# Attention's value products of two heads side by side in TensorE's columns, softmax sums as products of their own

## The chip, the cores and the metric

The kernel runs on one core of a Trainium2 chip. The metric is the device time of one execution in microseconds (us), as the median of several runs. Engines are named as in the profile: PE is TensorE (matmuls; PEld are its weight loads), DVE is VectorE, ACT is ScalarE, POOL is GpSimd, SP is SyncE, which here issues nearly all transfers (DMAs).

## The reference

Three layers follow each other. Inputs: 4 batches, 8 heads, 576 positions, 64 values a head; 32 heads in all.

```python
def _attn_ref(q, k, v, f):
    scores = scale * np.matmul(q, k.transpose(0, 1, 3, 2))
    cum = np.cumsum(np.log(np.clip(f, 0.0001, 1.0)), axis=-1)
    decay = cum[:, :, :, None] - cum[:, :, None, :]
    scores = np.where(causal, -1000000000.0, scores + decay)
    scores = scores - np.max(scores, axis=-1, keepdims=True)
    attn = np.exp(scores)
    attn = attn / (np.sum(attn, axis=-1, keepdims=True) + 1e-09)
    return np.matmul(attn, v)

def _moe_ref(x, w_in, w_spatial, b_spatial, w_out):       # x: heads side by side, 512 columns
    h = np.maximum(x @ w_in, 0.0)
    u, v = h[..., :512], h[..., 512:]
    v_n = (v - mean(v)) / np.sqrt(var(v) + 1e-06)
    v_s = np.einsum('ts,bsd->btd', w_spatial, v_n) + b_spatial[None, :, None]
    return (u * v_s) @ w_out

def _moe2_ref(x, mu_k, mu_r, w_k, w_v, w_r):
    xk, xr = mixes of x and x shifted by one position
    k = np.maximum(xk @ w_k, 0.0)
    return 1.0 / (1.0 + np.exp(-(xr @ w_r))) * (k * k @ w_v)
```

## The kernel before

Heads are worked in pairs: pair p holds heads 2p and 2p+1 (`g` is a head's number, 0 to 31). For each pair q and k are loaded, split into half-precision parts and transposed by DMA. For each head `score` and `rowmax` find the row maxima, and `scoreT` (L328) computes the scores once more, transposed, with keys on the partitions; ACT's exponential writes them to the tile `e`, 128 x 1600 f32. It holds, one behind the other, the five blocks of 128 keys (the last has 64), each with the queries that may see it: 576, 448, 320, 192 and 64 columns, starting at `EO`. `causal` (L341) clears on POOL what lies above the diagonal.

`pv` (L346) multiplies with the values, in f32. For each block c of keys, the stationary operand is 128 columns of the tile `v`, in which 64 columns of ones stand between the values of an even and of an odd head. So one product gives on 64 partitions of `o` the 64 outputs of the head, and on the other 64 its softmax sums. It is done in two halves of the queries, 0 to 255 (two products, of 256 and 128 columns) and 256 to 575 (five, of 320, 320, 320, 192 and 64). `o` is one PSUM tile of two banks, with one buffer, and serves one head.

`head` (L359) copies `o` to `xo` with ACT and sends the row of sums to the DRAM tile `rd`. Once a pair, `recip` (L370) brings the sums of both heads back with 9 to a partition, takes reciprocals on DVE, sends them to DRAM and spreads them over the partitions (`sr`). `norm` (L383) multiplies on POOL, one instruction a head; `xhi` and `xlo` split the result into two half-precision parts `xt`, on which the next layer's products work (m1v L504, m1u L558, m2 L575). These are done for batch b while the attention of batch b+1 runs; what is left of attention and of this layer runs out after 390 us, and from 445 us the last layers' products fill PE (L715).

Order: `plan_attention` (L611) gives each step a due time from the table `P` (L31), in units of a head, and a priority; the steps are written down in the order of these times, and a scheduler then settles the order of the instructions on each engine, while it keeps tiles and buffers free of conflicts. What it settles is fixed in the program. Due times of a head g are `pv` g+1.0 and g+1.3, `head` g+1.35; of a pair, counted from its odd head, `recip` 1.4, `norm` 1.9, `xhi` 2.2, `xlo` 2.4.

Of the kernel before, what the change touches and what calls it, by code (L numbers as in the profile page):

```python
# [29 lines left out]

P = dict(load=-8.0, sq=-5.6, ss=-5.2, sc=-5.0, hik=-4.6, lok=-4.25, hiq=-4.2, loq=-3.95, aux=-3.6,  # L31
         s=-2.4, m=-0.65, t=0.0, pv=1.0, out=1.35, rc=1.4, nr=1.9, xs=2.2, xl=2.4, mlp=2.7, mlplen=7.0, vload=-5.0, vsq=-3.0,
# [7 lines left out]
class K:  # L40
# [68 lines left out]
    def setup(self):  # L109
# [35 lines left out]
        self.v = [at.tile([128, 5, 4, 192], F32, name=f"v{i}") for i in range(2)]  # L145
# [19 lines left out]
    def init(self, i):  # L165

        g = self.nc.gpsimd
        if i < 3:
            for nm in ("kT", "kA"):
                g.memset(self.T[nm, i][:, 10], 0.0)  # L170
            t = self.T["kA", i].rearrange("p c t -> p (c t)")
            g.memset(t[64:69, 0:1280], MS)
            for h in range(2):
                g.memset(t[64:69, 640 * h:640 * h + 64], 0.0)
        elif i < 5:

            t = self.v[i - 3]
            x = g.memset(t[:, :, :, 64:128], 1.0)
            if i == 4:
                self.pin(x)  # L180
            g.memset(t[64:128, 4], 0.0)
        elif i == 5:
            for nm in "kq":
                g.memset(self.nat[nm, 2][0:64, :, 0, :], 0.0)
        else:
            self.pin(g.memset(self.xt[i - 6][:, :, 576:640], 0.0))
# [31 lines left out]
    def vload(self, b, c):  # L218
        t, src = self.v[b % 2], self.a["v"][b]
        t0, tn = KB[c]  # L220
        for e in range(2):
            self.nc.sync.dma_start(t[:tn, c, :, 128 * e:128 * e + 64], src[e::2, t0:t0 + tn].rearrange("h p d -> p h d"))

    def vsq(self, b, c):
        if c == 0:
            self.va = self.at.tile([128, 16], F32, tag="va", bufs=2, name="va")
        t = self.v[b % 2][:, c].rearrange("p a (x d) -> p a x d", d=64)[:, :, 0:3:2]
        self.sumsq(self.va[:, c:c + 1], t, self.junka[:, 0:512].rearrange("p (a x d) -> p a x d", a=4, x=2))
# [99 lines left out]
    def scoreT(self, g, u):  # L328
# [8 lines left out]
        if u == 0:  # L337
            self.e[g] = self.at.tile([128, 1600], F32, tag="e", bufs=2, name="e")
# [7 lines left out]
    def pv(self, g, hf):  # L346

        b, h = divmod(g, 8)
        if hf == 0:
            self.o[g] = self.pso.tile([128, 1024], F32, tag="o", name="o")  # L350
        o, e, v = self.o[g], self.e[g], self.v[b % 2]
        q0, q1 = ((0, 256), (256, 576))[hf]
        cs = [c for c in range(5) if KB[c][0] < q1]
        for c in cs:
            f = max(q0, KB[c][0])
            off = EO[c] + f - KB[c][0]
            self.nc.tensor.matmul(o[:, 256 + f:256 + q1], v[:, c, h // 2, 64 * (h % 2):64 * (h % 2) + 128], e[:, off:off + q1 - f], start=(c == 0), stop=(c == cs[-1]))  # L357

    def head(self, g):  # L359

        nc = self.nc
        o = self.o.pop(g)
        h = g % 2
        t = self.xo[h] = self.at.tile([128, 576], F32, tag="xo", bufs=3, name="xo")
        nc.scalar.copy(t, o[:, 256:832])
        if h == 0:
            self.rd = [self.hl.tile([2, 576], F32, tag=f"rd{i}", bufs=2, name=f"rd{i}") for i in range(2)]
        nc.sync.dma_start(self.rd[0][h:h + 1], t[64 - 64 * h:65 - 64 * h])
# [14 lines left out]
    def norm(self, p):  # L383

        self.xp = self.at.tile([128, 576], F32, tag="x", bufs=2, name="x")
        for h in range(2):
            r = slice(64 * h, 64 * h + 64)
            self.nc.gpsimd.tensor_tensor(self.xp[r], self.xo[h][r], self.sr[r], ALU.mult)  # L388
# [222 lines left out]
    def plan_attention(self):  # L611
# [21 lines left out]
        for g in range(G):  # L633
# [4 lines left out]
            for hf in range(2):  # L638
                add(g + P["pv"] + 0.3 * hf, 5, self.pv, g, hf)
            add(g + P["out"], 1, self.head, g)  # L640
            if g % 2:
                add(g + P["rc"], 1, self.recip, g // 2)
# [230 lines left out]
```

## Time and profile before

| | us |
|---|---|
| median of 3 runs | 752.72 (752.52 to 752.82) |
| profiled execution, first to last instruction | 750.9 |
| PE busy | 674.9 (90%) |
| DVE busy | 426.8 (57%) |
| ACT busy | 372.2 (50%) |
| POOL busy | 184.5 (25%) |
| L357, the value products on PE: 448 matmuls | 114.0 |
| L388, the norm's products on POOL: 32 | 47.0 |

The busy time of PE counts each matmul from its start to the end of its way through the array, so that the times of matmuls close behind each other overlap; what a matmul costs its successor is read from the distance of their starts. An f32 product is carried out as two matmuls (passes), each with its own weight load, so the 224 products of `pv` stand in the profile as 448.

### The profile page before, as it was taken

Reading aid. Unit: us, or ns where it says so; the run is one execution under the profiler, and the core shown is the slowest. Engines: PE = TensorE matmul, PEld = TensorE weight load, DVE = VectorE, ACT = ScalarE, POOL = GpSimd, SP = SyncE. Lnnn points to the kernel's source line nnn. Section 1 sums busy time; section 2 is a strip of 40 time slices with the busy share of each in tenths; the row PEclk is TensorE's granted clock in tenths of the full one; section 3 lists DMA queues with packets and bytes.
Section 4 is the critical chain, followed back from the end, with each engine's and each line's share of the span. In section 5 each row is a group of like instructions: output and inputs, shape, how many; then the busy total and the mean of one; then the engine's idle time right before and its main releaser. Section 6 shows DMA issues by size and latency. Waiting matters only on the chain.

```text
span 750.9 us, 11016 instructions
## 1 busy us (share of the span) xinstructions
PE 674.9 (90%) x3718; PEld 499.5 (67%) x3718; DVE 426.8 (57%) x1147; ACT 372.2 (50%) x740; POOL 184.5 (25%) x385
## 2 busy tenths in 40 slices
PE   0377878989998999999997679999999999999997
PEld 0245545647775677666774458788888888888886
DVE  5987786666655656646026879988225512632342
ACT  4626786666426854355505539747225412622431
POOL 7122645555324544445321201000000000000000
PEclk9998968999999999999999899999999999999999
DMA  9997666765655234410025453450100100010010
GB/s 228 203 204 158 168 138 131 147 137 107 126 133 122 56 71 99 97 27 18 18 64 184 146 192 124 140 164 15 42 27 16 57 0 15 1 56 1 1 57 28
DMA packets 130681, 69.78 MB, mean 93 GB/s; under 512 B 114704, under 2 KB 115312, under 8 KB 130624
## 3 DMA queue, kind: packets, MB, share of 16 engines
q1 hardware_dynamic: 128032, 67.89, 37.1%
q10 hardware_dynamic: 2592, 1.19, 0.7%
q8 instruction: 29, 0.48, 0.3%
q14 instruction: 28, 0.23, 0.1%
HBM read 42.06 MB, written 9.79 MB: 69 GB/s over the span
## 4 chain that ended last, share of the span: by engine, by line
PE 60%; DMA 16%; DVE 10%; POOL 5%; issue 3%; ACT 3%; SPq 1%; DVEq 0%; ACTq 0%; POOLq 0%
PE m L715 40%; PE o L357 7%; DMA sr<-rd 3%; POOL x L388 3%; PE m L575 3%; PE m1v L504 3%; PE s L302 3%; PE t L335 2%; PE m1u L558 2%; DMA rd<-r 2%; DVE junk L311 2%; DMA r<-rd 2%; DMA wst<-in_moe_w_k_dram 1%; DMA rd<-xo 1%; DMA wst<-in_moe_w_in_dram 1%
## 5 line engine op out<-in xcount | busy, mean ns | idle before, releaser
L357 PE MATMUL o<-e,v 128*128 128x320 f32 (+4 forms) x448 | 114.0, 384 | 5.5 <-POOL e L344 3.7
L715 PE MATMUL m<-xx,moe_w_k 128*128 128x512 f32 (+1 forms) x480 | 107.5, 373 | 0.4 <-ACT x L710 0.4
L715 PE MATMUL m<-moe_w_v,k 128*128 128x512 f32 x432 | 104.8, 391 | 0.0
L339 ACT ACTIVATE e<-t,qa 128x512 f32<-128x512 f32 (+1 forms) x128 | 72.6, 590 | 50.4 <-PE t L335 50.1
L311 DVE CUSTOM_DVE_ANT_0 junk<-s,mask 128x512 bf16<-128x512 f32 (+4 forms) x160 | 75.9, 474 | 37.8 <-PE s L302 32.2
L715 PEld LDWEIGHTS m<-xx,moe_w_k 128*128 128x128 f32 x480 | 84.0, 188 | 18.1 <-ACT x L710 0.9
L357 PEld LDWEIGHTS o<-e,v 128*128 128x128 f32 x448 | 78.5, 199 | 23.7 <-POOL e L344 6.1
L715 PEld LDWEIGHTS m<-moe_w_v,k 128*128 128x128 f32 x432 | 80.7, 188 | 17.7
L344 POOL TENSOR_SCALAR_AFFINE_SELECT e<-e 128x128 f32<-128x128 f32 (+1 forms) x160 | 52.2, 342 | 125.5 <-ACT e L339 123.0
L751 DVE TENSOR_TENSOR tmp<-tmp 128x512 f32<-128x512 f32 (+1 forms) x40 | 25.5, 638 | 88.1 <-ACT tmp L750 87.9
L302 PE MATMUL s<-kT,qT 128*128 128x512 f16 (+2 forms) x192 | 55.8, 299 | 21.6 <-DVE nm L311 13.7
L504 PE MATMUL m1v<-win,xt 128*128 128x512 f16 x240 | 61.5, 397 | 0.0
L388 POOL TENSOR_TENSOR x<-xo,sr 64x576 f32<-64x576 f32 x32 | 47.0, 1469 | 47.6 <-DMA sr<-rd 46.4
L715 PE MATMUL m<-gh,moe_w_out 128*128 128x512 f32 (+1 forms) x240 | 55.1, 380 | 3.5 <-DVE u L578 3.5
L335 PE MATMUL t<-qA,kA 69*128 69x512 f16 (+2 forms) x192 | 51.6, 294 | 7.3 <-DMA qA<-md 6.7
L558 PE MATMUL m1u<-xt,win 128*128 128x288 f16 x384 | 53.6, 286 | 4.5 <-ACT u L560 4.5
L750 ACT ACTIVATE tmp<-m 128x512 f32<-128x512 f32 (+1 forms) x40 | 22.1, 556 | 71.6 <-PE m L715 71.4
L575 PE MATMUL m<-wspT,vn 128*128 128x288 f16 x384 | 54.4, 290 | 3.0 <-DVE u L578 2.3
L302 PE MATMUL s<-kA,qA 67*128 67x512 f16 (+2 forms) x192 | 50.6, 300 | 4.0 <-DMA kA<-kT 3.7
L701 POOL COPY x<-x 128x4 f32<-128x4 f32 x4 | 3.5, 884 | 198.1 <-ACT x L710 198.1
L715 PEld LDWEIGHTS m<-gh,moe_w_out 128*128 128x128 f32 x240 | 43.3, 193 | 13.0 <-DVE u L578 3.8
L335 PE MATMUL t<-qT,kT 128*128 128x512 f16 (+2 forms) x192 | 51.4, 293 | 0.0
(159 smaller groups left out, 1083.8 us busy)
## 6 DMA issues: line engine op xcount, KB each, us to landing
sr<-rd SPq DMA_DIRECT2D x32, 144.0 KB
gd<-u SPq DMA_DIRECT2D x16, 288.0 KB
out_dram<-o SPq DMA_DIRECT2D x18, 256.0 KB
knat<-in_k_dram SPq DMA_DIRECT2D x32, 128.0 KB
v<-in_v_dram SPq DMA_DIRECT2D x32, 128.0 KB
g<-gd SPq DMA_DIRECT2D x16, 256.0 KB
wst<-in_moe_w_k_dram SPq DMA_DIRECT2D x8, 512.0 KB
wst<-in_moe_w_v_dram SPq DMA_DIRECT2D x8, 512.0 KB
```

The source lines that it names most:

```text
L302: self.nc.tensor.matmul(s[:, o:o + n], self.tok(qn, p, h, 128 * ib - 64, 128)[0:r], self.tok(kn, p, h, k0, n)[0:r], start=(j == 0), stop=( ...
L311: self.nc.vector.tensor_tensor_reduce(out=self.junk[r0:, 0:n], in0=self.s[u % 2][r0:, o:o + n], in1=self.mask[r0:, m0:m0 + n], op0=ALU.add ...
L335: self.nc.tensor.matmul(t[:, o:o + n], self.tok(kn, p, h, 128 * c, 128)[0:r], self.tok(qn, p, h, q0, n)[0:r], start=(j == 0), stop=(j == 1))
L339: self.nc.scalar.activation(self.e[g][:, 512 * u:512 * u + n], t[:, 0:n], AF.Exp, scale=self.qa[p][:, 5:6])
L344: self.nc.gpsimd.affine_select(out=e, in_=e, pattern=[[1, n]], compare_op=ALU.is_ge, fill=0.0, base=0, channel_multiplier=-1)
L357: self.nc.tensor.matmul(o[:, 256 + f:256 + q1], v[:, c, h // 2, 64 * (h % 2):64 * (h % 2) + 128], e[:, off:off + q1 - f], start=(c == 0), ...
L388: self.nc.gpsimd.tensor_tensor(self.xp[r], self.xo[h][r], self.sr[r], ALU.mult)
L504: nc.tensor.matmul(self.m1p, xt[:, xs, 128 * j:128 * j + 128], self.win[:, ws, kc, 512:1024], start=(kc == 0 and n == 0), stop=(kc == 3 an ...
L558: self.nc.tensor.matmul(o, self.win[:, ws, kc, fs], self.xt[(4 * b + kc) % 8][:, xs, ts_], start=(kc == 0 and n == 0), stop=(kc == 3 and n ...
L575: nc.tensor.matmul(o, pairs[n][0], pairs[n][1], start=(n == 0), stop=(n == 13))
L715: self.nc.tensor.matmul(out, l, r, start=(first and j == 0), stop=(last and j == len(pairs) - 1))
L751: nc.vector.tensor_tensor(tmp[:, 0:n], tmp[:, 0:n], tmp[:, 0:n], ALU.mult)
```

## The change

The two heads of a pair are now multiplied together, after the second one's exponentials. The values of a head are 64 stationary columns; head 2p is placed in the left half of the array's columns and writes partitions 0 to 63 of `o`, head 2p+1 in the right half and writes partitions 64 to 127. `o` holds a pair now. The softmax sums are products of their own: the stationary operand is 32 columns of ones, in one of four strips of 32 columns, two for each head. Which block, which queries and which place in `o` a strip works on stands in the table `SUMS`: each row is (block, first query, end, column of `o`), for strip j = 0 or 1 of a head. They use the columns of the two PSUM banks that the values leave free.

`e` has three buffers instead of two. `head` copies 864 columns once a pair, and four transfers bring the sums to `rd`. `norm` is one instruction on 128 partitions. `v` has no ones, and one transfer loads a block instead of two. The due times of `head`, `recip`, `norm`, `xhi` and `xlo` move back.

```diff
+SUMS = ((((0, 288, 480, 832),), ((1, 288, 480, 832),), ((2, 288, 480, 832),), ((3, 384, 480, 928),), ((0, 0, 96, 160),)),
+        (((0, 96, 288, 832),), ((1, 128, 288, 864),), ((0, 480, 576, 160), (1, 480, 576, 160)), ((2, 480, 576, 160),), ((3, 480, 576, 160),), ((4, 512, 576, 192),), ((2, 256, 288, 992),)))
...
-         s=-2.4, m=-0.65, t=0.0, pv=1.0, out=1.35, rc=1.4, nr=1.9, xs=2.2, xl=2.4, mlp=2.7, mlplen=7.0, vload=-5.0, vsq=-3.0,
+         s=-2.4, m=-0.65, t=0.0, pv=1.0, out=1.65, rc=1.7, nr=2.15, xs=2.35, xl=2.42, mlp=2.7, mlplen=7.0, vload=-5.0, vsq=-3.0,
...
-        self.v = [at.tile([128, 5, 4, 192], F32, name=f"v{i}") for i in range(2)]
+        self.v = [at.tile([128, 5, 8, 64], F32, name=f"v{i}") for i in range(2)]
...
-        for e in range(2):
-            self.nc.sync.dma_start(t[:tn, c, :, 128 * e:128 * e + 64], src[e::2, t0:t0 + tn].rearrange("h p d -> p h d"))
+        self.nc.sync.dma_start(t[:tn, c], src[:, t0:t0 + tn].rearrange("h p d -> p h d"))
...
-            self.e[g] = self.at.tile([128, 1600], F32, tag="e", bufs=2, name="e")
+            self.e[g] = self.at.tile([128, 1600], F32, tag="e", bufs=3, name="e")
...
-    def pv(self, g, hf):
-
-        b, h = divmod(g, 8)
-        if hf == 0:
-            self.o[g] = self.pso.tile([128, 1024], F32, tag="o", name="o")
-        o, e, v = self.o[g], self.e[g], self.v[b % 2]
-        q0, q1 = ((0, 256), (256, 576))[hf]
-        cs = [c for c in range(5) if KB[c][0] < q1]
-        for c in cs:
-            f = max(q0, KB[c][0])
-            off = EO[c] + f - KB[c][0]
-            self.nc.tensor.matmul(o[:, 256 + f:256 + q1], v[:, c, h // 2, 64 * (h % 2):64 * (h % 2) + 128], e[:, off:off + q1 - f], start=(c == 0), stop=(c == cs[-1]))
-
-    def head(self, g):
-
-        nc = self.nc
-        o = self.o.pop(g)
-        h = g % 2
-        t = self.xo[h] = self.at.tile([128, 576], F32, tag="xo", bufs=3, name="xo")
-        nc.scalar.copy(t, o[:, 256:832])
-        if h == 0:
-            self.rd = [self.hl.tile([2, 576], F32, tag=f"rd{i}", bufs=2, name=f"rd{i}") for i in range(2)]
-        nc.sync.dma_start(self.rd[0][h:h + 1], t[64 - 64 * h:65 - 64 * h])
+    def pv(self, p, part):
...
+        b = p // 4
+        mm = self.nc.tensor.matmul
+        if part == 0:
+            self.o[p] = self.pso.tile([128, 1024], F32, tag="o", name="o")
+        o, v = self.o[p], self.v[b % 2]
+
+        def probs(h, c, q0, q1):
+            off = EO[c] + q0 - KB[c][0]
+            return self.e[2 * p + h][:, off:off + q1 - q0]
+
+        if part < 2:
+            q0, q1 = ((0, 256), (256, 576))[part]
+            cs = [c for c in range(5) if KB[c][0] < q1]
+            for c in cs:
+                f = max(q0, KB[c][0])
+                for h in range(2):
+                    mm(o[64 * h:64 * h + 64, 256 + f:256 + q1], v[:, c, 2 * (p % 4) + h], probs(h, c, f, q1), start=(c == 0), stop=(c == cs[-1]))
+            return
+        ones = self.ones[:, 0:32]
+        for i in range(7):
+            for h in range(2):
+                for j in range(2):
+                    if j == 0 and i > 4:
+                        continue
+                    for c, q0, q1, at in SUMS[j][i]:
+                        r = 64 * h + 32 * j
+                        mm(o[r:r + 32, at:at + q1 - q0], ones, probs(h, c, q0, q1), start=(c == 0), stop=(q1 - 1) // 128 == c, tile_position=(0, r))
+
+    def head(self, p):
+
+        nc = self.nc
+        t = self.xo[p] = self.at.tile([128, 864], F32, tag="xo", bufs=2, name="xo")
+        nc.scalar.copy(t, self.o.pop(p)[:, 160:1024])
+        self.rd = [self.hl.tile([2, 576], F32, tag=f"rd{i}", bufs=2, name=f"rd{i}") for i in range(2)]
+        for r, q, n, at in ((0, 0, 96, 0), (32, 480, 96, 0), (0, 288, 192, 672), (32, 96, 192, 672)):
+            nc.sync.dma_start(self.rd[0][:, q:q + n], t[r:128:64, at:at + n])
...
-        for h in range(2):
-            r = slice(64 * h, 64 * h + 64)
-            self.nc.gpsimd.tensor_tensor(self.xp[r], self.xo[h][r], self.sr[r], ALU.mult)
+        self.nc.gpsimd.tensor_tensor(self.xp, self.xo.pop(p)[:, 96:672], self.sr, ALU.mult)
...
-            for hf in range(2):
-                add(g + P["pv"] + 0.3 * hf, 5, self.pv, g, hf)
-            add(g + P["out"], 1, self.head, g)
             if g % 2:
+                for part in range(3):
+                    add(g + P["pv"] + 0.2 * part, 5, self.pv, g // 2, part)
+                add(g + P["out"], 1, self.head, g // 2)
```

What this moves on PE, in the second batch's part of the program (pair 9, heads 18 and 19). Before, the end of head 19's products; `e_2595` is its tile of exponentials, `o_2767` its output, and a row with "x2" stands for two products:

```order
L302 LDWEIGHTS qA2_138
L302 MATMUL s_2818<-kA2_136,qA2_138 128x64
L357 MATMUL o_2767<-e_2595,v0_139 128x320 x2
L357 MATMUL o_2767<-e_2595,v0_139 128x192
L357 MATMUL o_2767<-e_2595,v0_139 128x64
L558 LDWEIGHTS win_103
```

After, at the same place of the program, the values of both heads; `e_2649` belongs to head 18, `e_2792` to head 19, and `o_2948` is the pair's output:

```order
L366 MATMUL o_2948<-e_2649,v0_139 64x320
L366 MATMUL o_2948<-e_2792,v0_139 64x320
L366 MATMUL o_2948<-e_2649,v0_139 64x320
L366 MATMUL o_2948<-e_2792,v0_139 64x320
L366 MATMUL o_2948<-e_2649,v0_139 64x192
L366 MATMUL o_2948<-e_2792,v0_139 64x192
L366 MATMUL o_2948<-e_2649,v0_139 64x64
L519 LDWEIGHTS xt6_147
```

And, some twenty matmuls of the next layer later, the beginning of the pair's sums:

```order
L376 MATMUL o_2948<-e_2649,ones_121 32x192 x2
L376 MATMUL o_2948<-e_2792,ones_121 32x192 x2
L376 MATMUL o_2948<-e_2649,ones_121 32x192
L376 MATMUL o_2948<-e_2649,ones_121 32x160
L376 MATMUL o_2948<-e_2792,ones_121 32x192
L376 MATMUL o_2948<-e_2792,ones_121 32x160
```

The products of the two heads now alternate, and the sums follow as a run of narrow products. Earlier in the same pair the first product, of 256 columns of head 18, stands alone between full-width matmuls of L335.

On SP's queue, before, the end of the same pair: two transfers of L368, of 576 sums each, with transposes and copies of other pairs between them, then the way through DRAM.

```order
L368 DMA rd_2669<-xo 1x576
L325 DMA md<-mr 20x128
L326 DMA qA_134<-md 2x1280
L272 DMA_TRANSPOSE kT_127<-nk 128x10x128
L272 DMA_TRANSPOSE qT_129<-nq 128x10x128
L278 DMA kA_128<-kT_127 64x1280
L279 DMA kA_128<-cumd 3x1280
L284 DMA qA_130<-qT_129 64x1280
L368 DMA rd_2669<-xo 1x576
L375 DMA r_2846<-rd_2669 128x9
L378 DMA rd_2670<-r_2846 128x9
L381 DMA sr<-rd_2670 64x576 x2
```

After, the same pair's sums:

```order
L385 DMA rd_3095<-xo 2x96 x2
L385 DMA rd_3095<-xo 2x192 x2
L392 DMA r_3106<-rd_3095 128x9
L395 DMA rd_3096<-r_3106 128x9
L398 DMA sr<-rd_3096 64x576 x2
```

All four transfers of a pair's sums now stand directly ahead of the one that waits for them.

## Rows read from the trace of the kernel before

**Rows 1.** The page's busy times, shares of the span and instructions of each engine.
```profile
PE 674.9 (90%) x3718; PEld 499.5 (67%) x3718; DVE 426.8 (57%) x1147; ACT 372.2 (50%) x740; POOL 184.5 (25%) x385
```
**Rows 2.** Three stretches: length, busy us and instructions by engine, granted clock, DMA.
```profile
core 0: us, PE busy (x) PEld busy (x) DVE busy (x) ACT busy (x) POOL busy (x), PEclk, DMA share, GB/s
0.00:125.00 125.00, 78.55 (x398) 49.84 (x399) 97.92 (x336) 76.89 (x167) 54.67 (x118) 0.90 0.82 177
125.00:400.00 275.00, 265.66 (x1750) 181.38 (x1749) 141.66 (x470) 136.40 (x279) 118.44 (x239) 0.98 0.42 92
400.00:751.00 351.00, 330.70 (x1573) 268.27 (x1571) 187.25 (x341) 158.90 (x294) 11.43 (x29) 0.99 0.19 64
```
**Rows 3.** Waits, 125 to 400 us: who for whom, total us, times, longest.
```profile
ACT e L339 <- PE t L335: 33.0, 29, 4.5
...
PE s L302 <- DVE nm L311: 3.5, 5, 2.3
...
PE o L357 <- POOL e L344: 2.4, 1, 2.4
...
PE t L335 <- ACT e L339: 0.2, 1, 0.2
```
**Rows 4.** The stretches again, line 357 alone: PE and PEld busy.
```profile
0.00:125.00 125.00, 32.29 (x112) 21.32 (x112) 0.90 0.82 177
125.00:400.00 275.00, 81.75 (x336) 57.15 (x336) 0.98 0.42 92
```
**Rows 5.** Timeline of PE from 347.2 us: start, us, line, operation, count.
```profile
347.30 0.19 PE L302 MATMUL s<-kT,qT 128*128 128x64 f16 x1
347.33 0.19 PE L302 MATMUL s<-kA,qA 67*128 67x64 f16 x1
347.36 2.35 PE L357 MATMUL o<-e,v 128*128 128x320 f32 x10
349.55 0.41 PE L558 MATMUL m1u<-xt,win 128*128 128x288 f16 x2
```
**Rows 6.** Timeline of PE from 261.9 us.
```profile
262.25 0.28 PE L71 MATMUL tot<-qa,ones 128*128 128x2 f32 x2
262.39 0.30 PE L302 MATMUL s<-kT,qT 128*128 128x320 f16 x1
```
**Rows 7.** Chain that ended last, from 378 us: start, us, what; the last pair.
```profile
384.94 2.87 DMA sr<-rd
387.82 0.07 issue
387.89 1.41 POOL x L388
389.30 0.07 issue
389.36 1.41 POOL x L388
390.77 0.02 issue
390.79 0.68 ACT xt L391
391.47 0.07 issue
391.54 1.29 POOL xt L395
```
**Rows 8.** ACT's group of the head's copy; SP's issue of the last sums.
```profile
L365 ACT COPY xo<-o 128x576 f32<-128x576 f32 x32 | 20.2, 633 | 26.0 <-PE o L357 22.3 <-POOL x L388 3.4
...
379.90 0.24 SPq L368 DMA_DIRECT2D rd<-xo  x1
```
**Rows 9.** Narrowest form of line 357: busy us, mean ns.
```profile
L357 PE MATMUL o<-e,v 128*128 128x64 f32 x64 | 11.0, 254 | 0.0
```

More of the change, by code (lines that the diff above doesn't have):

```diff
@@ L175, in init @@
         elif i < 5:
-            t = self.v[i - 3]
-            x = g.memset(t[:, :, :, 64:128], 1.0)
+            x = g.memset(self.v[i - 3][64:128, 4], 0.0)
             if i == 4:
                 self.pin(x)
-            g.memset(t[64:128, 4], 0.0)
         elif i == 5:
@@ L226, in vsq @@
             self.va = self.at.tile([128, 16], F32, tag="va", bufs=2, name="va")
-        t = self.v[b % 2][:, c].rearrange("p a (x d) -> p a x d", d=64)[:, :, 0:3:2]
-        self.sumsq(self.va[:, c:c + 1], t, self.junka[:, 0:512].rearrange("p (a x d) -> p a x d", a=4, x=2))
+        self.sumsq(self.va[:, c:c + 1], self.v[b % 2][:, c].rearrange("p h d -> p (h d)"), self.junka[:, 0:512])
     def vscale(self, b):
```

## The prediction

> **What bounds the kernel now.** I read the page's busy times first: TensorE (PE) is busy 90% of the span, the next engine 57% [rows 1]. A share over the whole span hides the stages, so the second view is the busy time of three stretches [rows 2]. Up to 125 us PE works 78.55 of 125 us and waits for loads and scaling. From 125 to 400 us it works 265.66 of 275 us at a granted clock of 0.98, and what it does wait for there is a handful of short waits, the longest group 3.5 us [rows 3]. After 400 us nothing of attention runs. So between 125 and 400 us attention is bounded by the columns that PE streams, and a microsecond added to PE or taken from it there moves the end of attention by about as much. The third view says how much of the changed line lies there: 336 of its 448 matmuls, 112 lie earlier [rows 4].
>
> What one of these matmuls costs must not be taken from its mean duration, since matmuls overlap in the pipeline. It is taken from starts. Every f32 product stands in the trace as two passes, each with its own weight load (448 for 224 products). Ten passes of one head (six of 320 columns, two of 192, two of 64: 2432 columns) start at 347.36 and the next line's matmul starts at 349.55 [rows 5]: 2.19 us, 0.90 ns a column. The full-width weight loads hide behind these streams. Starts are one behind the other in the order of the program, also where the second pass of a product follows its first.
>
> **Value products, L357.** Before, a head streams 1600 columns (256, 128, three of 320, 192, 64) twice: 3200, and 102,400 for 32 heads, times 0.90 ns = 92.2 us of PE. After, the same 102,400 columns are streamed, each into half of the array's columns. One at a time they cost 92.2 us again; two abreast 46.1 us.
>
> **Sums.** They came for nothing with the value products, as the 64 columns of ones beside v. Now they are 26 products a pair, 416 in all, 832 passes; the table's pieces add up to 768 + 832 = 1600 columns a head, so another 102,400 columns: 92.2 us one at a time, 46.1 us two abreast, 23.0 us four abreast.
>
> **How many abreast?** No row of before shows a matmul that leaves part of the array's columns free, so this is bounded from both sides: one at a time 184.4 us against 92.2 (+92.2), four abreast for the sums and two for the values 69.1 us (-23.1). I take two abreast for both. The reason is the order in which passes start: the second pass of a product goes into the same strip as its first, so it waits until that has streamed, and the product for the next strip stands behind it in the queue. What then runs together is the second pass of one product and the first of the next, two and never four. Net: 46.1 + 46.1 - 92.2 = 0.
>
> **Stretches.** Abreast needs a neighbour. The order of the changed kernel breaks its narrow products into 97 stretches with full-width matmuls between them, 21 of them of a single product; the first product of a stretch has 206 columns on average, and its first pass has nobody beside it: 97 x 206 x 0.90 ns = 18.0 us. In the pair shown, the values of 320 columns alternate well, while its first product of 256 stands alone.
>
> **Weight loads.** Passes narrower in columns but as many, and 832 more, bring 1280 loads for 448. Two passes of 2 columns, which hide no load, took 0.14 us from start to start of the next line [rows 6]; a pass of 64 columns behind another takes 0.03 us [rows 5], so a bare load of 128 columns is about 0.11 us. By columns (an estimate) 0.055 us for 64 and 0.028 us for 32. If the first load of each product waits for the pass before it to start, 224 x 0.055 + 416 x 0.028 = 24 us are added; if it is made early, nothing, as now behind the streams. I take the middle, 12 us.
> The Trainium skill (TensorE: Matmul & The Clock Gate, section Part 3, The mechanism) has it that a weight load overlaps matmuls in flight only where the row groups differ. All these loads use all rows, and yet rows 5 show them hidden; by that page of the skill the whole 24 us would stand, and the sum would come to about 789 us.
>
> **From PE time to the end.** 0 + 18 + 12 = 30 us more on PE. Three quarters (336 of 448) lie where PE is the bound and count in full, 22.5 us; of the quarter before 125 us, where PE idles a third of the time, I count half, 3.8 us. Together 26.3 us.
>
> **Head, norm, queues.** The last pair's chain goes on from PE: xo copy, four transfers, POOL's product, xt [rows 7]. POOL's two products of 64 partitions, 1.41 us each, become one of 128 with as many elements a partition; POOL's xt on 128x576 takes 1.29 us [rows 7], so one of about 1.4: -1.4 us. The copy grows from 576 to 864 columns, by 0.633 x 288/576 = 0.3 us at most [rows 8]. SP issues four transfers for two at the end of a pair, about 0.24 us each [rows 8]; three of them now stand before the recip's transfer: +0.7 us. Together -0.4 us, and only the last pair's counts; the earlier ones are covered by PE's own queue of projection work, and if that cover were gone each pair would show about as much. Twenty fewer v loads, fewer columns of memset and one copy for two on ACT lie on engines that are not the bound: nothing. The third e buffer lets a head's exponentials start while the pair before is still read: nothing either, since there ACT waits 33.0 us for PE's scores and PE 0.2 us for ACT [rows 3]; without it the pair's products would block.
> Sum: 750.9 (the profiled span) + 26.3 - 0.4 = 776.8 us; the median of the runs lies 1.8 us above that span (752.72), so **778 us**.
>
> **Rivals.**
> *Four abreast (faster).* If a waiting second pass doesn't hold back the strips behind it, sums run four abreast: -23.1 us, unaccompanied ends about half, 9 us, loads (832 x 0.028 = 23 us, as long as the streams) between 0 and 6 more. PE: -14 to -8, times 0.875 (three quarters in full, a quarter half): -12 to -7 us, 741 to 746, say 743 us. The place is the strips of L376 between 125 and 400 us; it decides from the point where 184.4/k + 18 + 12 falls under 92.2, at nearly three abreast, or 2.5 with all loads hidden. For it: the table turns through the four strips, so that four products in a row never share one. Against it: the two passes.
> The Trainium skill (same page, section Part 3, Measured speedup vs the span model) gives 2.38 times for three column strips of 512 columns; no row here shows one.
> *One at a time (the change doesn't do what it says).* +92.2 us and loads hidden as now: x 0.875 = +81, 833 us. Nothing in the trace speaks against it but that no pass there leaves columns free.
> *Emptying the array between widths.* The order has 206 places where a matmul of another column width follows. If the array has to run empty there, each costs what a pass lasts beyond its stream: a 64-column f32 pass lasts 254 ns [rows 9], less 58 ns of stream, so 0.2 us: 41 us, x 0.875 = +36 on the forecast, 814 us; with partial emptying from 795. Against it: passes of 128 and of 67 rows follow each other at 0.03 us [rows 5], but those differ in rows only.
> The Trainium skill (TensorEngine Tiling (Array Packing), section Key Properties) states that a change of tiling mode drains TensorE; by that page this rival is the rule, and no run here shows it.
>
> **How the numbers follow.** Two abreast without emptying 0.38: 762 to 794 (loads 0 to 24 us, 18 to 42 us of PE x 0.875 = 16 to 37, and some 6 us for other waits). Emptying 0.12 (795 to 822). One at a time 0.16 (822 to 850). Four abreast 0.34: 737 to 758, of which 0.25 faster, 0.06 the same, 0.03 slower. The likeliest is 778 us. About 0.2%, 1.5 us, is what a measurement of this kernel can tell from no change. Faster 0.25, same 0.06, slower 0.38 + 0.12 + 0.16 + 0.03 = 0.69. The range 740 to 812 leaves out one at a time (0.16), the top of emptying (0.03) and a corner of four abreast (0.03). Cases of both signs hold much of the chance, so the likeliest one's own range stands again: 762 to 794.
>
> **What would show it.** In the profile after: starts of the passes of L366 and L376. Two passes starting together and the next two a stream later is two abreast; four L376 starts within one stream is the first rival; starts one stream apart is the second. A gap of some 0.2 us before each change from L335, L519 or L573 to L366 is the third. Sums and values together should hold PE 120 us or so against 92. xo's copies should be 16, POOL's x 16 at about 1.4 us. Attention's last xt should land near 418 us instead of 392.8. If PE idles more than 20 us between 125 us and there for another engine, the argument that PE is the bound was wrong.

## The result and the profile after

The changed kernel takes 760.32 us (median of 4 runs, 757.99 to 762.34) where the kernel before takes 752.62 us beside it: 1.0108 times as long, 95% interval 1.0075 to 1.0141, so 7.7 us slower. The forecast had the sign, and its range (740 to 812) holds the time, but the range of the case that it held likeliest (762 to 794) begins above it, and it put the loss at 25 us, three times too much.

The page's busy times, the three stretches, and TensorE's waits from 125 to 400 us (who for whom, total us, times, longest), for the changed kernel, as in [rows 1 to 3]:
```profile
span 756.7 us, 12609 instructions
...
PE 685.8 (91%) x4550; PEld 481.8 (64%) x4550; DVE 417.6 (55%) x1147; ACT 368.2 (49%) x724; POOL 151.5 (20%) x367
...
0.00:125.00 125.00, 74.75 (x515) 42.23 (x515) 88.46 (x309) 71.41 (x153) 42.59 (x105) 0.88 0.79 167
125.00:400.00 275.00, 271.39 (x2413) 166.15 (x2413) 139.07 (x488) 136.18 (x275) 97.22 (x232) 1.00 0.42 91
400.00:751.00 351.00, 337.69 (x1619) 272.13 (x1617) 188.69 (x348) 160.65 (x297) 11.68 (x31) 0.98 0.21 66
...
PE s L302 <- DVE nm L311: 2.7, 3, 1.7
PE o L366 <- POOL e L344: 0.5, 1, 0.5
```
PE is busy 10.9 us more (685.8 against 674.9) in a span that is 5.8 us longer, so 5.1 us of its idle time went. From 125 to 400 us it now idles 3.6 us, against 9.3. Attention is bounded by PE, as the forecast said, but PE holds 11 us more work (5.4 in a second profile, below) and not 30.

Where the time goes can be read at the end of attention's last product. It comes at 379.20 us before and at 387.47 in the changed kernel (387.23 in the second profile). Up to there PE is busy 323.4 us before and 333.6 (329.7) after, and idle 55.8 and 53.9 (57.5). So in these profiles the 8 us by which attention's products end later are 6 to 10 us of PE's own work, and its idle time up to there is the same within 2 us.

The groups that answer to line 357 and to the copy and products of [rows 7, 8] (busy us, mean ns of one):
```profile
L366 PE MATMUL o<-e,v 128*64 128x320 f32 (+4 forms) x448 | 74.9, 393 | 3.0 <-POOL e L344 2.9
L376 PE MATMUL o<-e,ones 128*32 128x96 f32 (+4 forms) x832 | 34.2, 273 | 0.0
L403 POOL TENSOR_TENSOR x<-xo,sr 128x576 f32<-128x576 f32 x16 | 23.0, 1438 | 56.8 <-DMA sr<-rd 56.8
L382 ACT COPY xo<-o 128x864 f32<-128x864 f32 x16 | 14.0, 875 | 23.0 <-PE o L376 22.9
```
Busy times of matmuls overlap, so I count again from each start to the next start, less what PE stood idle between. Line 357 held PE for 98.9 us; now the values hold it for 70.2 and the sums for 31.7, together 101.9. The other 8 us lie in the full-width lines beside them (scores, their transposes, the projections and the spatial product): 273.7 us against 266.6.

The timeline of PE in the changed kernel shows both halves of the story (start, us, line, operation, count; where a row merges passes of several widths, it prints the first one's form):
```profile
183.60 0.76 PE L366 MATMUL o<-e,v 128*64 128x320 f32 x4
184.29 1.40 PE L573 MATMUL m1u<-xt,win 128*128 128x288 f16 x10
...
221.07 0.38 PE L335 MATMUL t<-qA,kA 69*128 69x512 f16 x1
221.29 0.38 PE L335 MATMUL t<-qT,kT 128*128 128x512 f16 x1
221.60 0.65 PE L366 MATMUL o<-e,v 128*64 128x256 f32 x2
222.18 0.38 PE L75 MATMUL tot<-qa,ones 128*128 128x2 f32 x2
...
225.36 0.25 PE L335 MATMUL t<-qA,kA 69*128 69x192 f16 x1
225.45 0.25 PE L335 MATMUL t<-qT,kT 128*128 128x192 f16 x1
225.62 0.65 PE L366 MATMUL o<-e,v 128*64 128x256 f32 x4
...
258.97 0.90 PE L573 MATMUL m1u<-xt,win 128*128 128x288 f16 x6
259.80 1.66 PE L376 MATMUL o<-e,ones 128*32 128x192 f32 x52
261.39 0.31 PE L335 MATMUL t<-qA,kA 69*128 69x320 f16 x1
...
261.85 0.90 PE L573 MATMUL m1u<-xt,win 128*128 128x288 f16 x6
262.58 0.38 PE L302 MATMUL s<-kT,qT 128*128 128x512 f16 x1
...
338.18 0.75 PE L366 MATMUL o<-e,v 128*64 128x320 f32 x2
338.86 0.82 PE L519 MATMUL m1v<-win,xt 128*128 128x512 f16 x3
```
- *Values, two abreast.* One product of 320 columns (two passes) that stands alone takes 0.68 us to the next line's start (338.18 to 338.86); two of them, one for each head, take 0.69 (183.60 to 184.29). The four passes at 225.62 are a product of 256 columns and, beside it, one of 128.
- *Sums, four abreast.* The 52 passes of a pair take 1.59 us. One strip streams at most 832 columns twice, which by the 0.90 ns a column of [rows 5] is 1.50 us; one after the other the four strips would take 5.76. Strip by strip the trace starts four first passes within 20 ns and the four second passes together 186 ns later. In this order, then, a second pass that waits for its strip does not hold up the strips behind it.
- *A change of width costs 0.1 us.* A pass of 512 f16 columns ahead of another takes 0.22 us (221.07), ahead of a narrow one 0.31 (221.29); with 192 columns 0.09 and 0.17; six passes of 288 columns take 0.73 us ahead of a full-width line (261.85) and 0.83 ahead of the sums (258.97). Over all 206 places the excess over a pass of the same form that no change follows is 96 to 99 ns in the median of every kind (from 128 columns to 64 or 32, from 64 to 32, and from both to 128). 206 x 0.097 = 20 us. Why a change costs this, the rows don't show.

### The profile page after: what moved, and what is told of

It reads as the page before. It is cut to its first block, busy times and chain, and to the rows that moved or that the text cites. A ratio compares the mean times of both kernels' runs of the same rounds, so it can differ in the third digit from the quotient of the medians.

```text
span 756.7 us, 12609 instructions
## 1 busy us (share of the span) xinstructions
PE 685.8 (91%) x4550; PEld 481.8 (64%) x4550; DVE 417.6 (55%) x1147; ACT 368.2 (49%) x724; POOL 151.5 (20%) x367
## 4 chain that ended last, share of the span: by engine, by line
PE 76%; DMA 8%; DVE 6%; SPq 2%; POOL 2%; ACT 2%; issue 1%; DVEq 0%; POOLq 0%; ACTq 0%
PE m L730 40%; PE o L366 7%; PE t L335 6%; PE m1v L519 5%; PE s L302 5%; PE m1u L573 5%; PE m L590 4%; PE o L376 3%; DMA sr<-rd 2%; DMA wst<-in_moe_w_k_dram 2%; DMA wst<-in_moe_w_in_dram 1%; DVE junk L311 1%; POOL x L403 1%; SPq L272 1%; DMA md<-mr 1%
## 5 line engine op out<-in xcount | busy, mean ns | idle before, releaser
L366 PE MATMUL o<-e,v 128*64 128x320 f32 (+4 forms) x448 | 74.9, 393 | 3.0 <-POOL e L344 2.9
L344 POOL TENSOR_SCALAR_AFFINE_SELECT e<-e 128x128 f32<-128x128 f32 (+1 forms) x160 | 48.8, 321 | 130.6 <-ACT e L339 129.4
L335 PE MATMUL t<-qA,kA 69*128 69x512 f16 (+2 forms) x192 | 52.2, 297 | 6.8 <-ACT e L339 4.3
L519 PE MATMUL m1v<-win,xt 128*128 128x512 f16 x240 | 57.6, 379 | 0.0
L366 PEld LDWEIGHTS o<-e,v 128*64 128x64 f32 x448 | 37.7, 144 | 26.3 <-issue 11.8
L335 PE MATMUL t<-qT,kT 128*128 128x512 f16 (+2 forms) x192 | 52.3, 298 | 0.0
L730 PE MATMUL m<-moe_w_r,xx 128*128 128x512 f32 x216 | 50.7, 392 | 0.0
L590 PEld LDWEIGHTS <-vn 128*128 128x128 f16 x384 | 37.0, 100 | 15.0 <-issue 2.3
```

Source lines behind the costliest of these rows:

```text
L335: self.nc.tensor.matmul(t[:, o:o + n], self.tok(kn, p, h, 128 * c, 128)[0:r], self.tok(qn, p, h, q0, n)[0:r], start=(j == 0), stop=(j == 1))
L344: self.nc.gpsimd.affine_select(out=e, in_=e, pattern=[[1, n]], compare_op=ALU.is_ge, fill=0.0, base=0, channel_multiplier=-1)
L366: mm(o[64 * h:64 * h + 64, 256 + f:256 + q1], v[:, c, 2 * (p % 4) + h], probs(h, c, f, q1), start=(c == 0), stop=(c == cs[-1]))
L519: nc.tensor.matmul(self.m1p, xt[:, xs, 128 * j:128 * j + 128], self.win[:, ws, kc, 512:1024], start=(kc == 0 and n == 0), stop=(kc == 3 an ...
L590: nc.tensor.matmul(o, pairs[n][0], pairs[n][1], start=(n == 0), stop=(n == 13))
L730: self.nc.tensor.matmul(out, l, r, start=(first and j == 0), stop=(last and j == len(pairs) - 1))
```

## The experiments

All are compared with the kernel before on the same chip; its medians there were 752.53 (first four), 752.57 (next four) and 750.49 us (last four). Single runs of it range from 747.85 to 756.65 us, so the 1.5 us that the forecast thought to tell from no change take many runs. In the first four expectations the theory is already that of the timeline above: products run abreast, a change of width costs 0.097 us.

**One unbroken run a pair.** All 40 narrow products of a pair stand together; the first waits for the odd head's last cut.
```diff
-                for part in range(3):
-                    add(g + P["pv"] + 0.2 * part, 5, self.pv, g // 2, part)
+                add(g + P["pv"], 5, self.pvrun, g // 2)
...
+    def pvrun(self, p):
+        self.pv(p, 0, True)
+        with self.tc.high_priority():
+            for part in range(3):
+                self.pv(p, part)
```


> The changed kernel with the 40 narrow products of a pair in one unbroken run (the first one waits for the last causal cut of the odd head, the others follow without a full-width matmul between): 16 stretches instead of 97, 48 changes of width instead of 206. Theory (narrow products do run side by side, two abreast for the values and four for the sums, and what eats the gain is some 0.1 us for each change of width plus products left alone): PE loses 158 x 0.097 = 15 us, 81 starts of a stretch x 0.047 = 4 us and some 14 us of products that ran alone, about 33 us less than the changed kernel, of which three quarters to nine tenths show: 730 to 737 us, faster than the kernel before. Rival 1 (the loss lies in the longer way from a pair's products to the next layer and in later due times): no gain, 757 to 763 us or later, since every pair's products now wait for the last cut. Rival 2 (products left alone cost it, changes of width cost nothing): about 14 + 4 us less PE, 743 to 748 us.

Measured: 767.22 us, ratio 1.0223 (1.0181 to 1.0265). PE's busy line, three rows of its timeline at one pair, and its longest waits from 40 to 400 us:
```profile
PE 665.3 (87%) x4550; PEld 482.6 (63%) x4550; DVE 420.8 (55%) x1147; ACT 366.4 (48%) x724; POOL 154.8 (20%) x367
...
165.36 2.92 PE L377 MATMUL o<-e,v 128*64 128x256 f32 x28
168.22 1.66 PE L390 MATMUL o<-e,ones 128*32 128x192 f32 x52
169.81 0.39 PE L335 MATMUL t<-qA,kA 69*128 69x512 f16 x1
...
PE s L302 <- DVE nm L311: 22.9, 22, 4.4
PE o L377 <- POOL e L344: 7.6, 5, 2.0
PE t L335 <- ACT e L339: 6.5, 8, 3.2
```
The stream is what the theory says: values 2.86 us a pair and sums 1.59 at full granted clock, 80.3 us for all with the slower first four pairs, and PE is busy 20.5 us less than in the changed kernel. The time is not: PE stands idle 99.5 us of the span (764.8 - 665.3) against 70.9. After 4.5 us without scores, the row minima on DVE come late, and the next scores wait for their buffers: the three waits above were 11.4, 2.9 and 4.3 us in the changed kernel, so they make 18.4 of the 28.5 us of idle time that were added. Of the expectations the theory's 730 to 737 us and the 743 to 748 fall; rival 1, which let every pair's products wait for the last cut, allowed this time. The forecast's working had PE as the only bound; taken from PE, time does not come back one for one.

**Narrow and full-width idle products in the kernel before.** 96 products of 32 columns whose results nobody reads, each between full-width matmuls, once with 32 columns of ones and once with 128.
```diff
+    def extra(self, t):
+        self.pin(self.nc.tensor.matmul(t[0:32, 300:332], self.ones[:, 0:32], self.ones[:, 0:32], start=True, stop=True))
```


> The kernel before with 96 idle products added (32 columns of ones times 32 columns of ones, into a part of a PSUM tile that nothing reads), each between full-width matmuls: after each head's last transposed scores and after each group of the next layer's two products. 192 changes of width. Theory (0.097 us for each change): PE 192 x 0.097 + 96 x 0.1 = 28 us more, of which 16 products lie after 400 us where PE is not the bound: 20 to 26 us more, 773 to 779 us. Rival (changes of width cost nothing, the loss has another cause): 96 x 0.1 us of passes, 5 to 9 us more, 757 to 762 us.

> The same 96 idle products in the kernel before, with 128 columns of ones instead of 32, so without a change of width. Theory: only passes and full-width weight loads, 96 x 0.14 us = 13 us on PE, of which 9 to 12 show: 762 to 765 us, and 10 to 16 us less than with 32 columns. Rival (changes of width cost nothing): as long as with 32 columns or longer, since the weight loads are longer.

Measured: 763.50 us narrow (1.018, 1.0132 to 1.0228), 775.97 us full-width (1.0346, 1.0288 to 1.0404). First the narrow kernel's timeline, then that of the full-width one:
```profile
173.91 1.63 PE L564 MATMUL m1u<-xt,win 128*128 128x288 f16 x12
175.48 0.25 PE L345 MATMUL m1u<-ones 128*32 128x32 f32 x2
175.66 0.26 PE L335 MATMUL t<-qT,kT 128*128 128x192 f16 x1
```
```profile
177.07 0.39 PE L345 MATMUL t<-ones 128*128 128x32 f32 x2
177.29 0.90 PE L363 MATMUL o<-e,v 128*128 128x256 f32 x4
...
184.51 1.63 PE L564 MATMUL m1u<-xt,win 128*128 128x288 f16 x12
185.98 0.30 PE L345 MATMUL m1u<-ones 128*128 128x32 f32 x2
186.12 0.22 PE L321 MATMUL mrow<-ident,nmh 128*128 128x128 f16 x1
```
The same twelve passes take 1.57 us ahead of the narrow product and 1.47 ahead of the full-width one: 0.10 us for the change, in a kernel that otherwise is the one before. A second change follows in the narrow product's own 0.18 us. The times miss both expectations, and in the wrong order. PE is busy about as much more in both (699.9 and 700.7): two full-width passes of 32 columns cost 0.14 us (185.98, as long as the two of 2 columns in [rows 6]) and 0.22 ahead of line 363 (177.07), so that the full-width products were no cheap control. The rest is idle time of PE, 61.6 us in the narrow kernel and 73.6 in the other; that it comes from the order that the scheduler then chose is likely, but not shown. So the price of a change stands on the rows, not on these two times.

**The kernel before with the later due times alone.**
```diff
-         ... out=1.35, rc=1.4, nr=1.9, xs=2.2, xl=2.4, ...
+         ... out=1.65, rc=1.7, nr=2.15, xs=2.35, xl=2.42, ...
```


> The kernel before with nothing but the later due times of the changed kernel for head, recip, norm, xhi and xlo. Theory (PE's columns are the bound): within 2 us of the kernel before, 751 to 755 us. Rival 1 (the later due times and the longer way to the next layer make the loss): 758 to 762 us.

Measured: 757.40 us, 1.0077 (1.0043 to 1.011), over the theory's 755 and just under the rival's 758. PE's work is the same (673.5 us busy, 674.9 before), its idle time is 82.5 us instead of 76.0. The order alone, without a changed instruction, moves this kernel by 5 us.

**The changed kernel with early due times.** The five due times of the head's end are put back or nearly so (1.45, 1.5, 1.95, 2.2, 2.4).

> The changed kernel with four due times put back near those of before (copy of the product 1.45 instead of 1.65, reciprocals 1.5 for 1.7, normalization 1.95 for 2.15, halves 2.2 and 2.4); products and changes of width stay (210 changes for 206). Theory A, that the later due times cost what they cost in the kernel before (+4.9 us there) and the stream of TensorE adds the rest: 755 us (753 to 757.5). Theory B, that the whole +7.7 us is TensorE's stream (changes of width and starts) and the due times only follow it: 760 (758.5 to 762).

Measured: 760.18 us, 1.0098 (1.0062 to 1.0133), like the changed kernel. Theory A falls: putting the due times back brings nothing here, though they cost 5 us in the kernel before.

**Early due times, and the sums in one stretch.**
```diff
...
+        if part in (2,):
+            with self.tc.high_priority():
+                for _ in ns:
+                    pass
```


> The kernel of the run above with the 26 sum products of a pair held together in one unbroken stretch; 160 changes of width for 210, the same products. Theory A, each change costs 0.097 us and TensorE's time counts by 0.875 as far as no new wait arises: 50 x 0.097 x 0.875 = 4.2 us less than the run above, 751 if that gives 755. Theory B, a longer stretch makes the scores wait as much as it saves (one run of 40 did): within 2 us of the run above or slower.

Measured: 756.83 us (11 runs), 1.0057 (1.0033 to 1.008). That is 3.4 us less than the run before for 50 changes of width fewer, where 4.2 were expected; but the intervals of the two overlap, so the gain is likely and not more. PE is busy 8.2 us less (675.3 against 683.5); 4.9 would be the changes, and the rest may be passes that no longer stand alone.

**Early due times, three gated stretches.** Parts 0 and 1 begin when the odd head's second and last cuts are done.

> The same early due times, the pair's narrow products in three stretches of 4, 10 and 26 (in places 4 and 36), each begun only when the last probabilities that it needs are there; 90 changes of width for 210. Theory A (changes are what is paid): 120 x 0.097 x 0.875 = 10.2 us less than the early kernel, about 745 (742 to 748). Theory B (the gates and stretches of 3 to 4 us make TensorE wait for the row minima afterwards, as the one-run kernel did at 767): 755 to 766, with 8 us or more of idle TensorE in 125 to 400 us.

Measured: 762.85 us, 1.0147 (1.0107 to 1.0188). Theory B: PE is busy only 667.8 us, but idle 93.2 of the span, 13.2 of it from 125 to 400 us.

**Strip after strip.** The same 26 products, written one strip after the other.
```diff
-        for i in range(7):
-            for h in range(2):
-                for j in range(2):
...
+        for h in range(2):
+            for j in range(2):
+                for i in range(5 + 2 * j):
```


> The changed kernel with the 26 sum products written strip after strip (5, 7, 5, 7 instructions) instead of in turn over the four strips; work and products the same, 210 changes of width. Theory A, a product can only start beside others that stand directly ahead of or behind it in the queue: the sums of a pair take about 4 times as long, 5.4 us for 1.4, 16 x 4.0 = 64 us of TensorE, x 0.875 = 56 us: 816 us (800 to 825). Theory B, every strip takes its products from a queue of its own, whatever their order: 760 us (757 to 764).

Measured: 800.00 us (one run). PE's busy line, the sums' group, and one pair's sums in the timeline:
```profile
PE 728.0 (91%) x4550; PEld 516.7 (65%) x4550; DVE 414.2 (52%) x1147; ACT 367.6 (46%) x724; POOL 153.8 (19%) x367
...
L374 PE MATMUL o<-e,ones 128*32 128x96 f32 (+4 forms) x832 | 84.0, 271 | 0.0
...
276.69 4.91 PE L374 MATMUL o<-e,ones 128*32 128x192 f32 x52
281.54 0.31 PE L335 MATMUL t<-qA,kA 69*128 69x320 f16 x1
```
A pair's 52 passes, unbroken, take 4.85 us here and took 1.59 above, both at a granted clock of 1.00. Over all pairs, broken ones included, the sums of a pair take 5.1 us from start to start against 2.0, 49.6 us more for all 16. Not all of it reaches the span: the values got 3.2 us shorter and the full-width lines 2.9. PE is busy 42.2 us more and the time is 39.7 longer, so theory A holds in its mechanism, if 16 us below its estimate: products run abreast only with their neighbours in the queue. The turn through the four strips in the table is what makes four abreast.

**Sums at most two abreast.** 64 columns of ones, in turn on the two halves.
```diff
-        ones = self.ones[:, 0:32]
+        ones = self.ones[:, 0:64]
...
+                    h = k % 2
+                    c, q0, q1, at = SUMS[j][i][k // 2]
+                    r = 64 * h
+                    mm(o[r:r + 64, at:at + q1 - q0], ones, probs(h, c, q0, q1), start=True, stop=True, tile_position=(0, r))
```


> The changed kernel with 64 columns of ones instead of 32 for every sum product, in turn on the two halves: the sums run at most two abreast by construction, the place of change of width between values and sums is gone but their number is 206 again. Every sum product here starts and ends its own accumulation and pieces overwrite each other, so the sums are left wrong. Theory A, that 32-column strips really run four abreast: the sums take twice as long, 23 us more of TensorE, 778 to 784 us, about where the forecast of two abreast was. Theory B, that the starts in the trace mislead and the strips share the array's time: 760 us (757 to 764).

Measured: 772.99 us (one run); the changed kernel, run beside it, 759.55. The sums' group:
```profile
L375 PE MATMUL o<-e,ones 128*64 128x96 f32 (+4 forms) x832 | 57.7, 276 | 0.0
```
From start to start the sums hold PE for 53.7 us, 22.0 more than in strips, as theory A has it to 1 us. The time rises by 13.4 us, less than its 18 to 24; the values are 5 us shorter in the new order. Theory B's 757 to 764 us falls. The ones are also twice as wide here, which this run alone doesn't separate from the strips; strip after strip, with 32 columns, does. This kernel has the sums as the forecast costed them, with changes of width besides.

**Three kernels side by side.** The changed kernel as it is; the same with its sums in one stretch (158 changes); and one with early due times, sums in one stretch and only the first value stretch gated (108 changes).

> The changed kernel once more, as it is, beside the three kernels below on one chip. Every theory: 760 us (758 to 762), TensorE busy 684 us or so.

> The changed kernel with one edit: the 26 sum products of a pair in one unbroken stretch, its due times as they are; 158 changes of width for 206. Theory A (changes at 0.097 us and lone first passes are what is paid, TensorE's time counts): 48 x 0.097 = 4.7 us and some 3 us of lone passes less on TensorE, 676 us busy, and 753 to 757 us for the whole. Theory B (what TensorE saves comes back as waits for the row minima and the exponentials): within 1.5 us of the changed kernel.

> Early due times, the sums in one unbroken stretch, and the first value stretch begun only when the odd head's second cut is done (so 9 products instead of 1, 2 and 6); the second value stretch is left free. 108 changes of width for 206. Theory A: 98 x 0.097 = 9.5 us and some 6 us of lone passes less on TensorE, 669 us busy; idle TensorE stays near the 55 to 62 us of the changed kernel and of the early one: 745 to 751 us. Theory B (as with three gated stretches): busy 668 us, idle 70 us or more, 757 to 764 us.

Measured: 759.55, 758.97 and 755.63 us; ratios 1.0138 (1.0076 to 1.0199), 1.0095 (1.0059 to 1.013) and 1.0069 (1.0042 to 1.0095). The busy lines of the three, in that order:
```profile
PE 680.3 (90%) x4550; PEld 478.5 (63%) x4550; DVE 416.1 (55%) x1147; ACT 367.9 (49%) x724; POOL 151.0 (20%) x367
```
```profile
PE 673.3 (89%) x4550; PEld 481.1 (64%) x4550; DVE 416.5 (55%) x1147; ACT 368.6 (49%) x724; POOL 150.9 (20%) x367
```
```profile
PE 668.8 (89%) x4550; PEld 479.6 (64%) x4550; DVE 416.9 (55%) x1147; ACT 364.2 (48%) x724; POOL 152.6 (20%) x367
```
PE's work falls as theory A says, by 7.0 and 11.5 us. The time falls by 0.6 and 3.9 us, and the intervals of all three overlap. The middle kernel alone speaks for theory B, but the same edit with early due times brought 3.4 us, so it doesn't settle it. In the last, whose time lies in neither theory's range, PE's idle time rises from 76.5 to 83.7 us; there theory A has PE's work right (668.8 for 669), and more idle time, as in theory B, goes with only a third of it arriving. The first kernel is also a caution: the same program showed PE busy 685.8 us in the first profile and 680.3 here, in spans of 756.7 and 756.8 us, most of the difference in the first 125 us (74.75 and 70.84) at granted clocks of 0.88 and 0.90. Differences of a few us in busy time between single profiles are not to be explained.

Busy and idle time of PE in the profiled runs (from the pages), and the medians of all runs:

| kernel | changes of width | PE busy | rest of the span | median us, ratio to before |
|---|---|---|---|---|
| before | 0 | 674.9 | 76.0 | 752.62 |
| changed | 206 | 685.8 | 70.9 | 760.32, 1.0108 |
| changed, again | 206 | 680.3 | 76.5 | 759.55, 1.0138 |
| early due times | 210 | 683.5 | 78.2 | 760.18, 1.0098 |
| sums in one stretch, early | 160 | 675.3 | 75.9 | 756.83, 1.0057 |
| sums in one stretch | 158 | 673.3 | 80.3 | 758.97, 1.0095 |
| first stretch gated, early | 108 | 668.8 | 83.7 | 755.63, 1.0069 |
| three gated stretches, early | 90 | 667.8 | 93.2 | 762.85, 1.0147 |
| one gated run | 48 | 665.3 | 99.5 | 767.22, 1.0223 |

No kernel here beats the one before. Fewer changes save PE's time. Where the stretches are gated to save them, PE's idle time grows; the sums in one stretch with early due times show no such growth.

## Why the prediction was right or wrong, point by point

- *What bounds the kernel:* right for what is added to PE, within limits. Strip after strip put 42 us on PE and 40 on the time. The full-width idle products put 25.8 on PE and 23.4 on the time, but the narrow ones 25.0 and 11: PE's idle time takes up some of the work in one order and less in another. Wrong for what is taken away: of 20.5 us less in the one-run kernel nothing arrived, and PE's waits for row minima, exponentials and cuts grew by 18.4 us.
- *Values, 46.1 us:* two abreast, right (0.68 us for one product of 320 columns, 0.69 for two).
- *Sums, 46.1 us:* the step that failed. "Two and never four" came from the idea that a second pass, waiting for its strip, blocks the queue behind it. The reason was half right: the queue does matter, as strip after strip shows, but four neighbours in four strips start together, and their second passes too. The term is 23.0, and the sums unbroken measured 1.59 x 16 = 25.4 us. The Trainium skill (TensorE: Matmul & The Clock Gate, section Part 3, Measured speedup vs the span model) gives 2.38 times for three column strips. Here a pair's sums, unbroken, take 1.59 us in turn over four strips against 4.85 strip after strip, 3.05 times.
- *Stretches 18 us and loads 12 us:* the first about right, the second did not show. The two lines hold PE 101.9 us; less 69.1 us of streams (46.1 + 23.0) and the 109 changes that end a stretch or lie inside one, at 0.097 (10.6 us), 22.2 us are left, where 30 were put. Line 357 before also held 6.7 us more than the 92.2 that the forecast set against them, 5.2 of it before 130 us, where the granted clock went down to 0.70 (100 to 125 us); the forecast took 0.90 ns a column throughout. The one-run kernel, which hardly has lone passes, leaves 80.3 - 69.1 - 32 x 0.097 = 8.1 us, and that is the clock again. Its values take 2.86 us a pair at a granted clock of 1.00, twelve times; the four stretches before 130 us take 4.54, 5.53, 4.89 and 5.53 at 0.50 to 0.62, 9.1 us more. One of them, with its stretch (0.50 is the lower level, 1.2 GHz; up to 125 us PE is busy 69.90 us):
```profile
83.74 5.60 PE L377 MATMUL o<-e,v 128*64 128x256 f32 x28 [2.04 <-POOL e L344]
...
83.70:89.20 5.50, 5.46 (x28) 3.09 (x28) 2.90 (x7) 1.54 (x4) 0.98 (x5) 0.50 0.67 156
```
  At 1.00 values and sums of a pair take 4.45 us, and 4864 columns at 0.90 ns and two changes would already be 4.57, so no time is left over for weight loads. In the changed kernel the values before 130 us hold PE 21.2 us for 25,600 columns and later 48.9 for 76,800; by that some 5 of the 22.2 us are the clock and some 17 (an estimate) lone passes and starts, near the 18. The rule of the Trainium skill on weight loads that the forecast weighed (TensorE: Matmul & The Clock Gate, section Part 3, The mechanism), by which 24 us would stand, is not borne out here; the same section also lets a load for the background weight buffer go ahead of matmuls in flight.
- *Changes of width, 0 us:* the other step that failed. It stood as a rival with a chance of 0.12 and a price of up to 0.2 us. The rule of the Trainium skill that was named there (TensorEngine Tiling (Array Packing), section Key Properties: a change of tiling mode drains TensorE) fits the rows, which put a price on a change though they don't show the draining itself: 0.097 us, 206 times, 20 us. The forecast took the price from how long a pass lasts beyond its stream, 0.2 us, twice too much.
- *The rivals were not exclusive.* Four abreast, and emptying between widths, were weighed as two cases, and both are true. The first gave -14 to -8 us of PE; with 20 us for the changes that is +6 to +12, and the two profiles of the changed kernel show +10.9 and +5.4. Times 0.875, less 0.4, on the median before: 757 to 763 us. Measured: 760.32. Both cases were in the text and were not added; but with its own price for a change (0.2 us, 41 us in all) PE would have had 27 to 33 us more and the sum been 776 to 781 us, so the price counts as much as the adding. That the sign came out right is in part luck: the sums were put 21 us too high and the changes 20 us too low, and the two nearly cancel.
- *Head, norm, queues, -0.4 us:* wrong by 3 us. The copy grew by 0.24 us as reckoned (875 ns for 633), and POOL's one product takes 1.44 us where the two took 2.82. But from the end of the last product to the start of the last xt it is 14.9 us (387.47 to 402.40), where it was 12.3 (379.20 to 391.54). The changed kernel's last pair:
```profile
385.81 1.66 PE L376 MATMUL o<-e,ones 128*32 128x192 f32 x52
387.50 0.88 ACT L382 COPY xo<-o 128x864 f32<-128x864 f32 x1 [4.57 <-PE o L376]
388.41 2.02 SPq L385 DMA_DIRECT2D rd<-xo  x4
392.15 0.76 SPq L392 DMA_DIRECT2D r<-rd  x1
400.22 1.41 POOL L403 TENSOR_TENSOR x<-xo,sr 128x576 f32<-128x576 f32 x1 [15.93 <-DMA sr<-rd]
402.40 1.28 POOL L410 TENSOR_TENSOR xt<-x,xt 128x576 f16<-128x576 f32 x1 [0.78 <-ACT xt L406]
```
  The four issues take 0.5 us each, not the 0.24 of [rows 8], which was the issue of a single row, and r<-rd starts 3.74 us behind the first of them, where it was 1.25 behind the one issue (379.90 to 381.15).
- *Signs to look for:* the last xt ended at 403.7 us, not near 418; sums and values hold 102 us, not 120; PE waits under 4 us from 125 to 400, as it should. The end moved less than attention did (by 10.9 us): after 400 us PE had 13.3 us of idle time, where it had 20.3.
- *What stays open:* how much of the 7.7 us is PE's and how much the order's. In the two profiles of the changed kernel PE's own work accounts for the later end of attention's products. But the order alone moved the kernel before by 5 us, undoing the due times brought nothing back, and halving the changes brought 4, with intervals that overlap. The kernel with PE's work under that before (668.8 us) is still 5 us slower. Its waits, as PE's for the exponentials from 40 to 400 us (7.1 us, before 0.6), are those of an order that the scheduler made up anew, and no run here separates this from the change itself.

## What to carry to other kernels

Matmuls on separate column strips ran abreast here, f32 with its two passes too, where neighbours in the queue stood on different strips; but each switch of the strip's width cost about a tenth of a microsecond, so count the switches in the real order before counting the columns. When two rivals don't exclude each other, add them, each at a price that a row shows. And where a second chain stands just behind the engine that bounds, as here, time added to that engine may be paid nearly in full (40 of 42 us) while time taken from it is not returned (0 of 20.5).

## What was not expected of the hardware

- A waiting second pass of an f32 product doesn't block the strips behind it: four first passes within 20 ns, four second passes 186 ns later; yet written strip after strip, a pair's 52 passes take 4.85 us where in turn they take 1.59.
- A change of column width costs 96 to 99 ns in every direction tried (128 to 64 or 32, 64 to 32, and 64 or 32 to 128), also around a single product of 32 columns. Changes of rows alone (128, 69, 67) show none of it (221.07 to 221.29, and [rows 5]).
- The order alone, with not one instruction changed, moved the kernel before by 5 us (757.40 against 752.53).
